# A gated attention/MLP mixer: attention products accumulated in w4's banks, and the gate computed once

## Chip, cores, metric

One core of a Trainium2 chip. The time is device microseconds of one execution on that core; a quoted time is the median of several executions, with the range beside it where it matters.

## The reference, cut

The output mixes a linear attention block A and an MLP block B over 2048 tokens of width 640, token by token, with a sigmoid gate:

```python
g = sigmoid((x * gate_w).sum(-1, keepdims=True))
a = A(x)     # phi(t) = where(t > 0, t + 1, exp(t)) + 1e-6;  o = (phi(q) kv) / (phi(q) z + 1e-6);  o @ wo
b = B(x)     # x1 = x + shift(gelu(LN(x) @ w1)) @ w2;  b = x1 + gelu(LN(x1) @ w3) @ w4
return g * a + (1 - g) * b
```

## The kernel before

The kernel records every operation, puts semaphore waits between the engines, and orders the work by a small timing model of its own: items such as ("k", 13), a key tile, or ("n1", 2), a normalisation, are emitted when the model says that they can run.

Five parts count here. The queries and keys go through `phi`. The clamp, the `ts` line, is a short VectorE operation on bf16 in SBUF:

```python
    def phi(b, dst, after_exp=None):
        se = slot("E", 3)
        src = psf[:, 512 * b:512 * b + D]            # a bank pair of PSUM
        activation(Er[:, se, :], src, ACTF.Exp)
        ...
        ts(dve, Er[:, se, :], Er[:, se, :], 1.0, EPS_PHI, ALU.min, ALU.add)       # the clamp
        return stt(dst, src, 1.0 + EPS_PHI, Er[:, se, :], ALU.add, ALU.max)       # frees the bank pair
```

The gate is computed for four tokens' tiles at a time, after the layer norm statistics of the same four, on ScalarE and GpSimd (POOL). POOL also runs the normalisations:

```python
    def gate_chunk(c):
        cs = slice(4 * c, 4 * c + 4)
        activation(stg[:, 1, cs], lr[:, cs, 1:2]..., ACTF.Tanh, scale=0.5)
        ts(pool, stg[:, 2, cs], stg[:, 1, cs], 0.5, 0.5, ALU.mult, ALU.add)     # g
        ts(pool, stg[:, 3, cs], stg[:, 1, cs], -0.5, 0.5, ALU.mult, ALU.add)    # 1 - g

    def normalize(which, t, st):
        ...
        ts(pool, xn[:, sx, :], x_tok[:, t, :], st[:, 6, t:t + 1], st[:, 7, t:t + 1], ALU.mult, ALU.add)
```

The attention product of a tile is made in a bank pair of its own and evicted at once into `abx`, which already holds (1 - g) x1:

```python
    def a_tile(t):
        ts(pool, abx[:, sa, :], x_tok[:, t, :], stg[:, 3, t:t + 1], 0.0, ALU.mult, ALU.add)
        b = pair()
        mm_group(ps[:, b, 0:512], [... 5 products of 512 columns])
        mm_group(ps[:, b + 1, 0:128], [... 5 products of 128 columns])
        stt(abx[:, sa, :], psf[...], stg[:, 2, t:t + 1], abx[:, sa, :], ALU.mult, ALU.add)
```

The w4 products then go to six fresh banks per chunk of four tiles; their eviction multiplies by 1 - g and adds `abx`. The w3 products of a chunk, 13 groups of five, rotate over all free banks, each group followed by a Gelu on ScalarE that frees its bank. (Cuts are marked with dots.)

Of the kernel before, what the change touches and what calls it, by code (L numbers as in the profile page):

```python
# [8 lines left out]
ALU = mybir.AluOpType  # L9
# [407 lines left out]
def _build(nc, A_x, A_wqkv, A_wo, B_w1, B_w2, B_w3, B_w4, gate_w, out, dbg=None, stop=None):  # L417
# [423 lines left out]
        tt(pool, st[:, 7, cs], st[:, 2, cs], st[:, 6, cs], ALU.mult)  # L841
        ts(pool, st[:, 7, cs], st[:, 7, cs], -1.0, 0.0, ALU.mult, ALU.add)

    def gate_chunk(c):
        cs = slice(4 * c, 4 * c + 4)
        activation(stg[:, 1, cs], lr[:, cs, 1:2].rearrange("p t o -> p (t o)"), ACTF.Tanh, scale=0.5)
        ts(pool, stg[:, 2, cs], stg[:, 1, cs], 0.5, 0.5, ALU.mult, ALU.add)
        ts(pool, stg[:, 3, cs], stg[:, 1, cs], -0.5, 0.5, ALU.mult, ALU.add)

    xn_slots = {}  # L850

# [85 lines left out]

    def stats1(c):
        ln_chunk_stats(st1, c, lr[:, 4 * c:4 * c + 4, 0:1].rearrange("p t o -> p (t o)"))
        gate_chunk(c)  # L940

    for u in range(NT):
        if u % 4 == 0:
            IT.add("S1", ("s1", u // 4), 0.0, lambda u=u: stats1(u // 4), deps=[(("k", u + 3), 1.8)])
        d1 = [(("s1", u // 4), 3.0 + 0.9 * (u % 4))]
        d1.append((("k", 13), 0.0) if u == 0 else (("n1", u - 1), 0.9))
        if u >= 3:
            d1.append((("t1", u - 3), 0.0))
        IT.add("N1", ("n1", u), 0.0, lambda u=u: normalize(1, u, st1), deps=d1)
        IT.add("T1", ("t1", u), 0.0, lambda u=u: t_xn(1, u), deps=[(("n1", u), 1.1)] + ([(("zb",), 0.0)] if u == 12 else []))  # L950
    for u in range(1, NT):
        IT.add("Z", ("z", u), 0.0, lambda u=u: z_add(u), deps=[(("k", NT - 1), 2.0)] if u == 1 else [])
    LAST_EXP = ("k", NT - 1)
# [156 lines left out]

    def qn_scale(t):
        sd = qn_slot[t]
        ts(dve, dnr[:, 0, sd, :], dnr[:, 0, sd, :], EPS_PHI, None, ALU.add, ALU.bypass)
        dve(lambda e: e.reciprocal(dnr[:, 1, sd, :], dnr[:, 0, sd, :]), [dnr[:, 0, sd, :]], [dnr[:, 1, sd, :]], cost=350.0)
        blk = pq_tok[:, t, :].rearrange("p (j c) -> p j c", c=128)
        src = pq_tok[:, t + 1, 0:600].rearrange("p (j c) -> p j c", c=120)
        rec = dnr[:, 1, sd, 0:30].rearrange("p (j a) -> p j a", a=6)
        halves = [(blk[:, :, 68 * e:68 * e + B3].rearrange("p j (a d) -> p j a d", d=DH),
                   src[:, :, 60 * e:60 * e + B3].rearrange("p j (a d) -> p j a d", d=DH),
                   rec[:, :, 3 * e:3 * e + 3].unsqueeze(3).to_broadcast([128, 5, 3, DH]), 450.0) for e in range(2)]  # L1120
        tail = (blk[:, :, 60:68].rearrange("p m (h i) -> p h m i", i=4),
                pq_tok[:, t + 1, 600:D].rearrange("p (h m i) -> p h m i", h=2, i=4),
                dnr[:, 1, sd, 30:32].unsqueeze(2).unsqueeze(3).to_broadcast([128, 2, 5, 4]), 150.0)
        for o, i0, i1, cost in (*halves, tail):
            dve(lambda e, o=o, i0=i0, i1=i1: e.tensor_tensor(o, i0, i1, ALU.mult),  # L1125
                [i0, dnr[:, 1, sd, :]], [o], cost=cost)
# [6 lines left out]
    def a_tile(t):  # L1133
        sa = slot("abx", 4)
        abx_slot[t] = sa
        tag_set("abx", sa, t)
        ts(pool, abx[:, sa, :], x_tok[:, t, :], stg[:, 3, t:t + 1], 0.0, ALU.mult, ALU.add)
        tok = slice(128 * t, 128 * (t + 1))
        b = pair()
        mm_group(ps[:, b, 0:512], [(pqnT[:, j, tok], M_sb[:, j, 0:512]) for j in range(KD)])  # L1140
        mm_group(ps[:, b + 1, 0:128], [(pqnT[:, j, tok], M_sb[:, j, 512:D]) for j in range(KD)])
        stt(abx[:, sa, :], psf[:, 512 * b:512 * b + D], stg[:, 2, t:t + 1], abx[:, sa, :], ALU.mult, ALU.add)

    w4_banks = {}

    def w4_half(t):
        sl = (t // 4) % 2
        tag_chk("h2T", sl, t // 4)
        b0, b2, bt = pair(), pair(), pair()
        tiles = [((b0, b2)[i // 2] + i % 2, bt + i % 2, 128 * (i // 2)) for i in range(4)]  # L1150
        for i in range(4):
            w4_banks[t + i] = tiles[i]
        bank_hold.update((b0, b0 + 1, b2, b2 + 1, bt, bt + 1))

        turned = t < NT - 4

        def fn(e):
            ins = None
            for pr in range(2):
                for par, tail in ((0, False), (1, False)) if turned else ((0, False), (1, False), (0, True), (1, True)):  # L1160
                    rows = slice(64 * par, 64 * par + 64)
                    bm, bs, q0 = tiles[2 * pr + par]
                    l = h2h[rows, t // 4, 128 * pr:128 * (pr + 1)]
                    if tail:
                        ins = e.matmul(ps[:, bs, q0:q0 + 128], l, w4[rows, KFF, 512:D], start=(pr == 0), stop=False,
                                       skip_group_check=True)
                    else:
                        ins = e.matmul(ps[:, bm, :], l, w4[rows, KFF, 0:512], start=True, stop=False)  # L1168
            if turned:
                for par in range(2):  # L1170
                    rows = slice(64 * par, 64 * par + 64)
                    ins = e.matmul(ps[:, bt + par, 0:256], w4[rows, KFF, 512:D], h2h[rows, t // 4, :], start=True, stop=False)  # L1172
            return ins
        pe(fn, [h2h[:, t // 4, :], w4[:, KFF, :]], [ps[:, b, :] for b in (b0, b0 + 1, b2, b2 + 1, bt, bt + 1)], cost=760.0)

    def w4_turned(t):
        sl = (t // 4) % 2
        tag_chk("h2T", sl, t // 4)
        tag_set("mtok", sl, t // 4)
        bt = w4_banks[t][1]  # L1180
        for par in range(2):
            o = ps[:, bt + par, 0:256].rearrange("p (n q) -> p n q", q=128)
            prs = [(w4[:, k, 512:D], h2T[:, sl, k, :].rearrange("p (n h q) -> p n h q", h=2, q=128)[:, :, par, :]) for k in range(KFF)]

            def fn(e, o=o, prs=prs):
                ins = None
                for i, (l, r) in enumerate(prs):
                    ins = e.matmul(o, l, r, start=False, stop=(i == KFF - 1))  # L1188
                return ins
            pe(fn, [x_ for p_ in prs for x_ in p_], [o], cost=KFF * 109.2)  # L1190
            activation(mT[:, sl, :].rearrange("p (n h q) -> p n h q", h=2, q=128)[:, :, par, :], o, ACTF.Copy)
        bank_hold.difference_update((bt, bt + 1))
        sch.dma("sp", mtok[:, sl, :, :], mT[:, sl, :], "trm%d" % sl, transpose=True)

    def w4_tile(t):
        sa = abx_slot[t]
        tag_chk("abx", sa, t)
        sl = (t // 4) % 2
        tag_chk("h2T", sl, t // 4)
        a = t % 4  # L1200
        b1, b2, q0 = w4_banks.pop(t)

        def grp(o, n0, n1):
            prs = [(h2T[:, sl, k, 128 * a:128 * (a + 1)], w4[:, k, n0:n1]) for k in range(KFF)]

            def fn(e):
                ins = None
                for i, (l, r) in enumerate(prs):
                    ins = e.matmul(o, l, r, start=False, stop=(i == KFF - 1), skip_group_check=(n0 > 0))  # L1209
                return ins  # L1210
            pe(fn, [x_ for p_ in prs for x_ in p_], [o], cost=KFF * ((n1 - n0) * 0.4167 + 2.5))
        parts = [(ps[:, b1, 0:512], 0, 512)]
        if t >= NT - 4:
            parts.append((ps[:, b2, q0:q0 + 128], 512, D))
        for o, n0, n1 in parts:
            grp(o, n0, n1)
        bank_hold.discard(b1)
        if t < NT - 4:
            tag_chk("mtok", sl, t // 4)
            parts.append((mtok[:, sl, a, :], 512, D))  # L1220
        elif a >= 2:
            bank_hold.discard(b2)
        for o, n0, n1 in parts:
            stt(x_tok[:, t, n0:n1], o, stg[:, 3, t:t + 1], abx[:, sa, n0:n1], ALU.mult, ALU.add)
# [16 lines left out]
    for c in range(NCH):  # L1241
        for j in range(KD):
            deps = [(("t1", u), 0.9) for u in range(4 * c, 4 * c + 4)] if j == 0 else []
            if c == 0 and j == 0:
                deps.append((LAST_EXP, None))
                deps.append((("ga", KD - 1), None))
            if c == 1 and j == 0:
                deps.append((("g", KD - 1), None))
# [41 lines left out]
                    IT.add("W3", ("w3h", c2), 1.14, lambda c2=c2: w3_half(c2), [(("t2", u), 0.9) for u in range(4 * c2 + 4, 4 * c2 + 8)] + [(("a", 3), 0.0)])  # L1290
                IT.add("W3", ("w4h", 0), 0.76, lambda: w4_half(0), [(("w4load",), 0.0)])
    for t in range(NT):
        deps = [(("zb",), 1.0), (("q", max(t, 2)), 2.0)]
        if t < 7:
            i = (5 * t) // 2 + 3
            deps.append((("w1", i // KD, i % KD), 0.0))
# [9 lines left out]
    for t in range(NT):  # L1306
# [7 lines left out]
        deps4 = [(("a", t), 0.0), (("w3h", c - c % 2), GEL), (("w3", c, KFF - 1), GEL)]  # L1314
        if t % 4 == 0:
            deps4.append((("w3", min(c + 1, NCH - 1), KFF - 1), 0.0))
            if t == 0:
                deps4 = [(("w4h", 0), 0.0)]
        elif t + 3 < NT:
            deps4.append((("a", t + 3), 0.0))  # L1320
# [56 lines left out]
```

## Time and profile before

| | before |
|---|---|
| median of the first three executions | 260.15 us (259.63 to 260.22) |
| span of the profiled execution | 258.4 us |
| TensorE busy | 255.2 us |
| first input product / last w4 product of 512 columns done | 7.15 / 255.69 us |

From the page of before, the busy time of the engines (share of the span, instructions):

```profile
PE 255.2 (99%) x1600; PEld 130.5 (51%) x1600; DVE 151.3 (59%) x290; ACT 109.6 (42%) x223; POOL 93.9 (36%) x152
```

From the same page, the chain of work that ended last, by engine:

```profile
PE 96%; DMA 2%; SPq 0%; DVE 0%; issue 0%
```

A busy TensorE can still stall, so the waits of TensorE itself are the better reading. From the list of waits of before (who waited for whom: total us, times, longest), the longest one of VectorE, and all that the matmuls have; these two lie at the very start:

```profile
DVE x_tok L642 <- PE ps L1209: 62.0, 13, 18.9
...
PE ps L871 <- PEq L1362: 0.8, 1, 0.8
...
PE ps L614 <- DMA x_tok<-in_A_x_dram: 0.2, 1, 0.2
```

So the TensorE is never kept waiting once the first input has landed, and only fewer or cheaper products can shorten the kernel. The groups that the change touches, from the list of groups by shape (line, engine, operation, output and input, count; busy us, mean ns; idle time before):

```profile
L642 DVE SCALAR_TENSOR_TENSOR abx<-ps,stg,abx 128x640 f32<-128x640 f32 x16 | 14.1, 883 | 15.8 <-PE ps L603 8.8 <-POOL abx L625 7.0
L625 DVE TENSOR_SCALAR Er<-Er 128x640 bf16<-128x640 bf16 x32 | 11.6, 363 | 8.1 <-ACT Er L659 8.0
L625 POOL TENSOR_SCALAR stg<-stg 128x4 f32<-128x4 f32 x8 | 1.9, 263 | 0.7 <-ACT stg L659 0.7
L659 ACT ACTIVATE stg<-lr 128x4 f32<-128x4 f32 x4 | 0.8, 203 | 0.0
```

The first goes away, the last two are replaced. The second is not in the change.

```profile
45.79 0.34 POOL L625 TENSOR_SCALAR stg<-stg 128x4 f32<-128x4 f32 x2 [0.50 <-ACT stg L659]
46.07 0.95 POOL L285 DMA_DIRECT2D wv<-in_A_wqkv_dram  x1
47.02 3.28 POOL L285 DMA_DIRECT2D wo_aug<-in_A_wo_dram  x5
50.35 1.80 POOL L625 TENSOR_SCALAR xn<-x_tok,st 128x640 bf16<-128x640 bf16 x2
```

The Gelus of w3 of chunk 2, from the timeline of ScalarE in before (start us, duration us, engine); 0.48 us of idle time between 0.60 us of work:

```profile
175.13 0.60 ACT L659 ACTIVATE h2T<-ps 128x512 bf16<-128x512 f32 x1 [0.48 <-PE ps L603]
176.21 0.60 ACT L659 ACTIVATE h2T<-ps 128x512 bf16<-128x512 f32 x1 [0.48 <-PE ps L603]
```

### The profile page before, as it was taken

The numbers are of one execution on the slowest core, as the hardware profiler recorded it, in microseconds if no ns is written. First come the engines' busy times: TensorE is split into PE (matmuls) and PEld (weight loads), VectorE is DVE, ScalarE is ACT, GpSimd is POOL, SyncE is SP. The second block draws the span as 40 slices with busy tenths as digits, with TensorE's granted clock in tenths as the row PEclk, the third lists the DMA queues.
The fourth block names the chain that finished last, engine by engine and source line by source line (L and its number), as shares of the span: only waits on it lengthen the run. The fifth ranks groups of instructions, "written<-read, shape, count | busy, mean of one in ns | idle before, by whom it ended". The sixth has DMA issues, their size and how long they took to land.

```text
span 258.4 us, 4134 instructions
## 1 busy us (share of the span) xinstructions
PE 255.2 (99%) x1600; PEld 130.5 (51%) x1600; DVE 151.3 (59%) x290; ACT 109.6 (42%) x223; POOL 93.9 (36%) x152
## 2 busy tenths in 40 slices
PE   8999999999999999999999999999999999999996
PEld 3555555544454554555444555444465444644453
DVE  2587877899914999999993403995004410044333
ACT  1496677751366866676854240005510045300000
POOL 5013995969952118767903202222002110012001
PEclk9999999999999999999999999999999999999999
DMA  6764999682764898562825651115010020010211
GB/s 217 215 154 136 208 183 137 178 131 51 100 128 80 152 405 258 65 103 51 105 59 115 123 70 20 28 25 152 0 23 0 0 101 3 0 20 3 103 51 51
DMA packets 54307, 25.86 MB, mean 100 GB/s; under 512 B 45668, under 2 KB 52877, under 8 KB 54288
## 3 DMA queue, kind: packets, MB, share of 16 engines
q1 hardware_dynamic: 52112, 21.21, 37.4%
q0 software_dynamic: 1168, 3.28, 5.7%
q10 hardware_dynamic: 1008, 1.11, 1.2%
q8 instruction: 12, 0.20, 0.3%
q14 instruction: 7, 0.06, 0.1%
HBM read 12.04 MB, written 2.62 MB: 57 GB/s over the span
## 4 chain that ended last, share of the span: by engine, by line
PE 96%; DMA 2%; SPq 0%; DVE 0%; issue 0%
PE ps L603 61%; PE ps L1209 18%; PE ps L805 8%; PE ps L1188 3%; DMA x_tok<-in_A_x_dram 2%; PE ps L898 2%; PE ps L1096 1%; PE ps L1168 1%; SPq L285 0%; PE ps L899 0%; DVE x_tok L642 0%; PE ps L977 0%; PE ps L1006 0%; PE ps L614 0%; PE ps L1172 0%
## 5 line engine op out<-in xcount | busy, mean ns | idle before, releaser
L603 PE MATMUL ps<-xnT,w 128*128 128x512 bf16 x360 | 81.3, 380 | 0.0
L659 ACT ACTIVATE h2T<-ps 128x512 bf16<-128x512 f32 x52 | 30.5, 598 | 60.4 <-PE ps L603 60.4
L603 PEld LDWEIGHTS ps<-xnT,w 128*128 128x128 bf16 x360 | 34.2, 98 | 38.3 <-issue 0.3
L625 POOL TENSOR_SCALAR abx<-x_tok,stg 128x640 f32<-128x640 bf16 x16 | 14.8, 925 | 99.7 <-DVE x_tok L642 94.6
L1209 PE MATMUL ps<-w,h2T 128*128 128x512 bf16 (+1 forms) x260 | 50.1, 348 | 0.0
L642 DVE SCALAR_TENSOR_TENSOR x_tok<-ps,stg,abx 128x512 bf16<-128x512 f32 (+1 forms) x20 | 13.3, 670 | 62.0 <-PE ps L1209 62.0
L625 POOL TENSOR_SCALAR xn<-x_tok,st 128x640 bf16<-128x640 bf16 x32 | 35.3, 1110 | 17.8 <-DMA xnT<-xn 17.3
L1209 PEld LDWEIGHTS ps<-w,h2T 128*128 128x128 bf16 x260 | 22.9, 98 | 22.1 <-issue 0.3
L659 ACT ACTIVATE Er<-ps 128x640 bf16<-128x640 f32 x32 | 22.5, 708 | 15.0 <-PE ps L603 8.0
L658 ACT ACTIVATE junk<-x_tok 128x640 bf16<-128x640 bf16 x32 | 23.6, 739 | 3.4 <-DVE x_tok L640 2.8
L603 PE MATMUL ps<-M_sb,pqnT 128*128 128x512 bf16 (+1 forms) x160 | 24.4, 300 | 0.0
L659 ACT ACTIVATE hsT<-ps 128x512 bf16<-128x512 f32 (+1 forms) x32 | 19.0, 593 | 12.1 <-PE ps L603 11.6
L603 PE MATMUL ps<-w,hsT 128*128 128x512 bf16 (+1 forms) x160 | 23.7, 300 | 0.0
L642 DVE SCALAR_TENSOR_TENSOR abx<-ps,stg,abx 128x640 f32<-128x640 f32 x16 | 14.1, 883 | 15.8 <-PE ps L603 8.8
L603 PE MATMUL ps<-wkg,xT 128*128 128x130 bf16 (+1 forms) x140 | 21.4, 299 | 0.0
L603 PEld LDWEIGHTS ps<-M_sb,pqnT 128*128 128x128 bf16 x160 | 13.6, 98 | 13.0
L603 PE MATMUL ps<-wq,xT 128*128 128x512 bf16 (+1 forms) x130 | 19.8, 300 | 0.0
L603 PEld LDWEIGHTS ps<-w,hsT 128*128 128x128 bf16 x160 | 13.3, 98 | 12.3
L805 PE MATMUL ps<-pk_tok,x_tok 128*128 128x512 bf16 x80 | 17.8, 380 | 0.0
L625 DVE TENSOR_SCALAR Er<-Er 128x640 bf16<-128x640 bf16 x32 | 11.6, 363 | 8.1 <-ACT Er L659 8.0
L1125 DVE TENSOR_TENSOR pq_tok<-pq_tok,dnr 128x300 bf16<-128x300 bf16 (+1 forms) x48 | 15.7, 381 | 0.6
L640 DVE SCALAR_TENSOR_TENSOR x_tok<-ps,x_tok 128x640 bf16<-128x640 f32 x16 | 13.1, 820 | 4.5 <-PE ps L603 3.8
(84 smaller groups left out, 250.6 us busy)
## 6 DMA issues: line engine op xcount, KB each, us to landing
w<-in_B_w_dram SPq DMA_DIRECT2D x1, 2160.0 KB, 8.3
w<-in_B_w_dram SPq DMA_DIRECT2D x1, 2080.0 KB, 13.9
out_dram<-x_tok SPq DMA_DIRECT2D x3, 640.0 KB, 3.1
x_tok<-in_A_x_dram SPq DMA_DIRECT2D x2, 640.0 KB, 5.0
w<-in_B_w_dram POOLq DMA_DIRECT2D x8, 160.0 KB, 4.5
x_tok<-in_A_x_dram SPq DMA_DIRECT2D x5, 160.0 KB, 4.9
wv<-in_A_wqkv_dram POOLq DMA_DIRECT2D x1, 800.0 KB, 6.7
wq<-in_A_wqkv_dram ACTq DMA_DIRECT2D x4, 160.0 KB, 4.1
```

The lines of the kernel that those rows point to most:

```text
L603: ins = e.matmul(out_ap, l, r, start=(i == 0), stop=(i == n - 1))
L625: return engf(lambda e: e.tensor_scalar(out_ap, in_ap, s1, s2, op0, op1), rd, [out_ap], cost=cost)
L640: return dve(lambda e: e.scalar_tensor_tensor(out_ap, in0, scalar, in1, op0, op1, accum_out=accum), rd, [out_ap, accum], cost=cost + 70.0)
L642: return dve(lambda e: e.scalar_tensor_tensor(out_ap, in0, scalar, in1, op0, op1), rd, [out_ap], cost=cost)
L658: return act(lambda e: e.activation(out_ap, in_ap, func, bias=bias, scale=scale, accum_out=accum), rd, wr, cost=cost)
L659: return act(lambda e: e.activation(out_ap, in_ap, func, bias=bias, scale=scale), rd, wr, cost=cost)
L805: ins = e.matmul(o, l, r, start=(t0 + q_ == 0), stop=(t0 + q_ == NT - 1))
L898: e.matmul(ps[:, b, 0:512], l, w[:, k, 0:512], start=(k == 0), stop=(k == KD - 1))
L1096: ins = e.matmul(o, l, r, start=st, stop=sp)
L1125: dve(lambda e, o=o, i0=i0, i1=i1: e.tensor_tensor(o, i0, i1, ALU.mult), [i0, dnr[:, 1, sd, :]], [o], cost=cost)
L1188: ins = e.matmul(o, l, r, start=False, stop=(i == KFF - 1))
L1209: ins = e.matmul(o, l, r, start=False, stop=(i == KFF - 1), skip_group_check=(n0 > 0))
```

## The change

The intent is to save the 16 evictions into `abx`. Since g a + (1 - g)(x1 + h2) = (1 - g)(x1 + h2 + (g / (1 - g)) a), and g / (1 - g) is exp of the gate logit, the queries are scaled by that factor (the denominator is multiplied by exp of minus the logit), the attention products are left in the banks where w4's products accumulate, and one eviction does the rest. The gate itself is then needed late, so its math is done once for all tokens, behind the z sums (the sums of phi(k) over the tokens, for the denominator). The core of the diff:

```diff
-    def gate_chunk(c):                       # per four tiles: Tanh on ACT, two operations on POOL
-        ...
+    def gate_clip():
+        ts(dve, stg[:, 1, :], lr[:, :, 1:2]..., LOGIT, -LOGIT, ALU.min, ALU.max)
+    def gate_exp():
+        activation(stg[:, 2, :], stg[:, 1, :], ACTF.Exp, scale=-1.0)
+    def gate_rest():
+        ts(dve, stg[:, 0, :], stg[:, 2, :], 1.0, None, ALU.add, ALU.bypass)
+        dve(lambda e: e.reciprocal(stg[:, 1, :], stg[:, 0, :]), ...)
+        tt(dve, stg[:, 3, :], stg[:, 2, :], stg[:, 1, :], ALU.mult)
...
     def stats1(c):
         ln_chunk_stats(st1, c, ...)
-        gate_chunk(c)
...
+    IT.add("SG", ("sgc",), 0.0, gate_clip, deps=[(("k", NT - 1), 1.0)])
+    IT.add("SG", ("sg", 0), 0.0, gate_exp, deps=[(("sgc",), 0.2)])
+    IT.add("SG", ("sg", 1), 0.0, gate_rest, deps=[(("z", NT - 1), 0.0)])
...
-        ts(dve, dnr[:, 0, sd, :], dnr[:, 0, sd, :], EPS_PHI, None, ALU.add, ALU.bypass)
+        ts(dve, dnr[:, 0, sd, :], dnr[:, 0, sd, :], EPS_PHI, stg[:, 2, t:t + 1], ALU.add, ALU.mult)
...
     def a_tile(t):
-        b = pair()
-        mm_group(...); mm_group(...)
-        stt(abx[:, sa, :], psf[...], stg[:, 2, t:t + 1], abx[:, sa, :], ALU.mult, ALU.add)
+        b = w4_banks[t] = bank()
+        bank_hold.add(b)                     # held until the last w4 product of this tile
+        acc([(ps[:, b, :], [... 5 products of 512 columns])], True)
+        if t >= NT - 4: ...                  # tails of 128 columns, as before
+        elif i == 3:                         # tails of four tiles, turned: 2 x 5 products of 256 columns
+            ...
...
-                        ins = e.matmul(ps[:, bm, :], l, w4[rows, KFF, 0:512], start=True, stop=False)
+                        ins = e.matmul(ps[:, bm, :], l, w4[rows, KFF, 0:512], start=False, stop=False, ...)
...
+            deps4.append((("a", t + 3), 0.0))        # w4 of a chunk waits for all four attention tiles
```

More of the change, by code (lines that the diff above doesn't have):

```diff
@@ L842, in ln_chunk_stats @@
         ts(pool, st[:, 7, cs], st[:, 7, cs], -1.0, 0.0, ALU.mult, ALU.add)
-    def gate_chunk(c):
-        cs = slice(4 * c, 4 * c + 4)
-        activation(stg[:, 1, cs], lr[:, cs, 1:2].rearrange("p t o -> p (t o)"), ACTF.Tanh, scale=0.5)
-        ts(pool, stg[:, 2, cs], stg[:, 1, cs], 0.5, 0.5, ALU.mult, ALU.add)
-        ts(pool, stg[:, 3, cs], stg[:, 1, cs], -0.5, 0.5, ALU.mult, ALU.add)
+    LOGIT = 60.0
+    def gate_clip():
+        ts(dve, stg[:, 1, :], lr[:, :, 1:2].rearrange("p t o -> p (t o)"), LOGIT, -LOGIT, ALU.min, ALU.max)
+    def gate_exp():
+        activation(stg[:, 2, :], stg[:, 1, :], ACTF.Exp, scale=-1.0)
+    def gate_rest():
+        ts(dve, stg[:, 0, :], stg[:, 2, :], 1.0, None, ALU.add, ALU.bypass)
+        dve(lambda e: e.reciprocal(stg[:, 1, :], stg[:, 0, :]), [stg[:, 0, :]], [stg[:, 1, :]])
+        tt(dve, stg[:, 3, :], stg[:, 2, :], stg[:, 1, :], ALU.mult)
     xn_slots = {}
@@ L1138, in a_tile, with acc, fn @@
         tok = slice(128 * t, 128 * (t + 1))
-        b = pair()
-        mm_group(ps[:, b, 0:512], [(pqnT[:, j, tok], M_sb[:, j, 0:512]) for j in range(KD)])
-        mm_group(ps[:, b + 1, 0:128], [(pqnT[:, j, tok], M_sb[:, j, 512:D]) for j in range(KD)])
-        stt(abx[:, sa, :], psf[:, 512 * b:512 * b + D], stg[:, 2, t:t + 1], abx[:, sa, :], ALU.mult, ALU.add)
+        i = t % 4
+        b = w4_banks[t] = bank()
+        bank_hold.add(b)
+        acc([(ps[:, b, :], [(pqnT[:, j, tok], M_sb[:, j, 0:512]) for j in range(KD)])], True)
+        if t >= NT - 4:
+            if i == 0:
+                for par in range(2):
+                    bt = w4_tails[3, par] = bank()
+                    bank_hold.add(bt)
+            acc([(ps[:, w4_tails[3, i % 2], 128 * (i // 2):128 * (i // 2) + 128],
+                  [(pqnT[:, j, tok], M_sb[:, j, 512:D]) for j in range(KD)])], i < 2)
+        elif i == 3:
+            c = t // 4
+            for par in range(2):
+                bt = w4_tails[c, par] = bank()
+                bank_hold.add(bt)
+                acc([(ps[:, bt, 0:256].rearrange("p (n q) -> p n q", q=128),
+                      [(M_sb[:, j, 512:D], pqnT[:, j, 512 * c:512 * (c + 1)].rearrange("p (n h q) -> p n h q", h=2, q=128)[:, :, par, :])
+                       for j in range(KD)])], True)
+    def acc(groups, first=False, last=False):
+        for o, prs in groups:
+            def fn(e, o=o, prs=prs):
+                ins = None
+                for i, (l, r) in enumerate(prs):
+                    ins = e.matmul(o, l, r, start=first and i == 0, stop=last and i == len(prs) - 1, skip_group_check=True)
+                return ins
+            pe(fn, [x_ for p_ in prs for x_ in p_], [o], cost=len(prs) * (nfree(prs[0][1]) * 0.4167 + 2.5))
+    w4_tails = {}
     w4_banks = {}
@@ L1148, in w4_half @@
         tag_chk("h2T", sl, t // 4)
-        b0, b2, bt = pair(), pair(), pair()
-        tiles = [((b0, b2)[i // 2] + i % 2, bt + i % 2, 128 * (i // 2)) for i in range(4)]
-        for i in range(4):
-            w4_banks[t + i] = tiles[i]
-        bank_hold.update((b0, b0 + 1, b2, b2 + 1, bt, bt + 1))
+        c = t // 4
+        tiles = [(w4_banks[t + i], w4_tails[c, i % 2], 128 * (i // 2)) for i in range(4)]
+        banks = [w4_banks[t + i] for i in range(4)] + [w4_tails[c, par] for par in range(2)]
         turned = t < NT - 4
@@ L1164, in fn @@
                     if tail:
-                        ins = e.matmul(ps[:, bs, q0:q0 + 128], l, w4[rows, KFF, 512:D], start=(pr == 0), stop=False,
+                        ins = e.matmul(ps[:, bs, q0:q0 + 128], l, w4[rows, KFF, 512:D], start=False, stop=False,
                                        skip_group_check=True)
                     else:
-                        ins = e.matmul(ps[:, bm, :], l, w4[rows, KFF, 0:512], start=True, stop=False)
+                        ins = e.matmul(ps[:, bm, :], l, w4[rows, KFF, 0:512], start=False, stop=False, skip_group_check=True)
             if turned:
@@ L1171, in fn @@
                     rows = slice(64 * par, 64 * par + 64)
-                    ins = e.matmul(ps[:, bt + par, 0:256], w4[rows, KFF, 512:D], h2h[rows, t // 4, :], start=True, stop=False)
+                    ins = e.matmul(ps[:, tiles[par][1], 0:256], w4[rows, KFF, 512:D], h2h[rows, t // 4, :], start=False, stop=False,
+                                   skip_group_check=True)
             return ins
-        pe(fn, [h2h[:, t // 4, :], w4[:, KFF, :]], [ps[:, b, :] for b in (b0, b0 + 1, b2, b2 + 1, bt, bt + 1)], cost=760.0)
+        pe(fn, [h2h[:, t // 4, :], w4[:, KFF, :]], [ps[:, b, :] for b in banks], cost=760.0)
     def w4_turned(t):
@@ L1179, in w4_turned @@
         tag_set("mtok", sl, t // 4)
-        bt = w4_banks[t][1]
         for par in range(2):
-            o = ps[:, bt + par, 0:256].rearrange("p (n q) -> p n q", q=128)
-            prs = [(w4[:, k, 512:D], h2T[:, sl, k, :].rearrange("p (n h q) -> p n h q", h=2, q=128)[:, :, par, :]) for k in range(KFF)]
-            def fn(e, o=o, prs=prs):
-                ins = None
-                for i, (l, r) in enumerate(prs):
-                    ins = e.matmul(o, l, r, start=False, stop=(i == KFF - 1))
-                return ins
-            pe(fn, [x_ for p_ in prs for x_ in p_], [o], cost=KFF * 109.2)
+            bt = w4_tails[t // 4, par]
+            o = ps[:, bt, 0:256].rearrange("p (n q) -> p n q", q=128)
+            acc([(o, [(w4[:, k, 512:D], h2T[:, sl, k, :].rearrange("p (n h q) -> p n h q", h=2, q=128)[:, :, par, :]) for k in range(KFF)])],
+                last=True)
             activation(mT[:, sl, :].rearrange("p (n h q) -> p n h q", h=2, q=128)[:, :, par, :], o, ACTF.Copy)
-        bank_hold.difference_update((bt, bt + 1))
+            bank_hold.discard(bt)
         sch.dma("sp", mtok[:, sl, :, :], mT[:, sl, :], "trm%d" % sl, transpose=True)
@@ L1200, in w4_tile @@
         a = t % 4
-        b1, b2, q0 = w4_banks.pop(t)
-        def grp(o, n0, n1):
-            prs = [(h2T[:, sl, k, 128 * a:128 * (a + 1)], w4[:, k, n0:n1]) for k in range(KFF)]
-            def fn(e):
-                ins = None
-                for i, (l, r) in enumerate(prs):
-                    ins = e.matmul(o, l, r, start=False, stop=(i == KFF - 1), skip_group_check=(n0 > 0))
-                return ins
-            pe(fn, [x_ for p_ in prs for x_ in p_], [o], cost=KFF * ((n1 - n0) * 0.4167 + 2.5))
+        b1 = w4_banks.pop(t)
         parts = [(ps[:, b1, 0:512], 0, 512)]
         if t >= NT - 4:
-            parts.append((ps[:, b2, q0:q0 + 128], 512, D))
+            b2 = w4_tails[3, a % 2]
+            parts.append((ps[:, b2, 128 * (a // 2):128 * (a // 2) + 128], 512, D))
         for o, n0, n1 in parts:
-            grp(o, n0, n1)
+            acc([(o, [(h2T[:, sl, k, 128 * a:128 * (a + 1)], w4[:, k, n0:n1]) for k in range(KFF)])], last=True)
         bank_hold.discard(b1)
@@ L1245, in _build @@
                 deps.append((LAST_EXP, None))
+                deps.append((("sg", 0), None))
                 deps.append((("ga", KD - 1), None))
@@ L1292, in _build @@
     for t in range(NT):
-        deps = [(("zb",), 1.0), (("q", max(t, 2)), 2.0)]
+        deps = [(("zb",), 1.0), (("q", max(t, 2)), 2.0), (("sg", 1), 0.0)]
         if t < 7:
```

## The prediction

> **What bounds the kernel now.** The TensorE. The page says busy 255.2 of 258.4 us, but a busy PE may stall, so I read start-to-start times in the timeline: 13 products of 512 columns take 2.80 us (0.216 each), an attention group (five of 512, five of 128) 1.36 us (1.08 + 0.28, so 0.056 per short one), 26 turned products of 256 columns 2.94 us (0.113). The Trainium skill ("TensorE: Matmul & The Clock Gate", "Wait — 56ns, not 53.3ns?") gives 55.6 and 215.7 ns for a warm array; this trace agrees. The chain of waits is 96% PE: from 7.15 us (first input landed) to 255.69 us products back to back. Only about seven steps, where the row layout of the array changes, take 0.31 instead of 0.22 us.
>
> **What the change removes, adds, moves.**
> - TensorE: no column goes. 12 attention groups keep their five 512-column products; their tails turn from 60 products of 128 columns (60 x 0.056 = 3.36 us) into 30 of 256 (3.3 to 3.4 us). Net about zero.
> - VectorE: the 16 evictions into abx go (14.1 us, 883 ns each, by groups). In the w4 stages VectorE waits for PE (62.0 us in the waits), and no product waits for an abx eviction: worth nothing on the chain.
> - Gate: four Tanh (0.8 us of ACT) and eight POOL operations (1.9 us) become one Exp and four small VectorE operations (estimated from the 128x32 ones, 0.25 to 0.35 us: 1 us). Behind the z sums VectorE waits 5.2 us for the z transpose. Table loads stay two: the skill's "ScalarE: Activation LUTs", "Table sets", puts exp and tanh in one set; the groups show two loads. PE is then in GT products. Worth nothing.
> - PSUM: the attention result now holds its bank from the attention product to the last w4 product. In w3 of chunks 2 and 3 six of eight banks are held, so 26 w3 groups (28 us) rotate on two banks. The new hazard: a Gelu starts 0.20 us after its group's last column and takes 0.60: the bank is free 0.80 us after the group; it is needed at 1.08, its first weight load at 0.87. ACT has nothing else there. The slack (0.07 to 0.28 us) is just enough, I think. A later release costs up to 0.1 us per group, at most 2.4 us.
> - Order: w4's half products wait for all four attention tiles. Earlier chunks met that already; tile 15 moves from before w4(15) to before w4(12), and its transposed queries landed at 181 us, long before. No gap.
>
> **On the critical path:** about zero gained, 0 to 2 us at risk.
>
> **Predicted time:** 260.2 us, range 259.3 to 261.5. Faster by over 2%: 1%. Within 2%: 95%. Slower by over 2%: 4%.
>
> **What would show it right.** PE busy near 255 us, span 258 to 259; VectorE down about 13 us to near 138; two table loads; w4 groups at 2.80 us; w3 of chunks 2 and 3 at 14.03 us per 65 products, starts still 0.216 apart. Wrong: steps over 0.26 us every fifth product there, PE or its weight load waiting for ACT's Gelu; or turned attention tails far from 0.11 us each.
>
> **What would make it wrong.** A bank release later than the Gelu's recorded end; a VectorE backlog in chunk 0's w4 (query scaling plus evictions) that delays a held bank; a new order of the early products that opens a gap by the z row or the gate.

## More of the kernel before

```profile
49.49 0.40 DVE L625 TENSOR_SCALAR Er<-Er 128x640 bf16<-128x640 bf16 x1 [0.39 <-ACT Er L659]
49.92 0.82 DVE L642 SCALAR_TENSOR_TENSOR pq_tok<-ps,Er 128x640 bf16<-128x640 f32 x1
50.86 0.55 DVE L625 TENSOR_SCALAR Er<-Er 128x640 bf16<-128x640 bf16 x1
```

These lines of POOL and of VectorE are from the timeline late in the query and key stage: POOL waits 0.50 us for the Tanh, makes the gate, issues six transfers of weights (DMA) and then runs two normalisations. A clamp issued while POOL normalises took 0.55 us; most take 0.33.

## The result

| | before | after |
|---|---|---|
| median, six executions each | 259.85 us (259.07 to 260.22) | 261.03 us (260.33 to 261.79) |
| ratio, 95% interval | | 1.0048 (1.0025 to 1.0071) |
| span of the profiled execution | 258.4 us | 259.6 us |
| VectorE busy | 151.3 us | 141.1 us |

The outputs are correct. The kernel became slower, by half a per cent: small, but the interval leaves out zero.

The answering lines of after: busy times and chain from its page, then the same waits: VectorE's longest and all that the matmuls have.

```profile
PE 254.2 (98%) x1542; PEld 130.9 (50%) x1570; DVE 141.1 (54%) x278; ACT 109.5 (42%) x220; POOL 91.8 (35%) x144
```

```profile
PE 88%; DVE 6%; DMA 2%; ACT 2%; issue 1%; SPq 0%
```

```profile
DVE x_tok L642 <- PE ps L1173: 90.3, 14, 22.1
...
PE ps L878 <- PEq L1381: 0.8, 1, 0.8
PE ps L603 <- DVE pq_tok L642: 0.7, 1, 0.7
...
PE ps L603 <- issue: 0.2, 1, 0.2
PE ps L1173 <- issue: 0.2, 1, 0.2
```

There are 1542 matmuls for 1570 weight loads: 28 matmul records are missing from this trace, and the two waits for "issue" of 0.2 us are such holes. The 0.7 us wait for VectorE's `pq_tok` is none: the weight load before it is late as well, by the list of waits of the weight loads:

```profile
PEld ps L603 <- DVE pq_tok L642: 0.9, 1, 0.9
```

Most of VectorE's 6% in the chain lies between 83 and 96 us, where TensorE loses nothing against before (third and fourth line of the table below). To see where the time went I cut every trace at five weight loads that each kernel has: the first with the key weights, the first of the kv products, the first and last of the products with Lt (kv times wo, in the middle of w1 and w2), and the first of w4's half products.

| stage (us) | before | after | difference, before rounding |
|---|---|---|---|
| start to first key product | 9.86 | 10.22 | +0.36 |
| keys, queries, G products | 66.63 | 67.51 | +0.88 |
| kv, first w1 and w2 products | 16.60 | 16.60 | 0.00 |
| w1, w2, start of w3 | 31.94 | 31.94 | 0.00 |
| w3 | 27.60 | 27.58 | -0.03 |
| first half product of w4 to the end | 105.82 | 105.78 | -0.05 |

The last two stages, which hold all the accumulation work, are 0.07 us shorter together. The first line is the arrival of the first inputs and differs from execution to execution whatever the kernel: it ranged from 9.12 to 11.30 us over all profiles. The second line is the loss. Here is its place, in the chain that ended last in after, between 48 and 53 us (start us, us, what):

```profile
47.94 1.16 PE ps L603 x9
...
49.12 0.71 ACT Er L659
...
49.86 2.02 DVE Er L625
...
51.91 0.84 DVE pq_tok L642
...
52.79 1.54 PE ps L603 x10
```

A key product waits for a bank pair, that waits for the queries' eviction, and that for a clamp of 2.0 us, six times its usual length. The timelines of POOL and then of VectorE in after, at the same place as above:

```profile
45.67 0.95 POOL L285 DMA_DIRECT2D wv<-in_A_wqkv_dram  x1
46.63 3.28 POOL L285 DMA_DIRECT2D wo_aug<-in_A_wo_dram  x5
49.96 2.65 POOL L625 TENSOR_SCALAR xn<-x_tok,st 128x640 bf16<-128x640 bf16 x3
```

```profile
49.86 2.01 DVE L625 TENSOR_SCALAR Er<-Er 128x640 bf16<-128x640 bf16 x1 [0.44 <-ACT Er L659]
51.91 0.82 DVE L642 SCALAR_TENSOR_TENSOR pq_tok<-ps,Er 128x640 bf16<-128x640 f32 x1
52.65 0.32 DVE L625 TENSOR_SCALAR Er<-Er 128x640 bf16<-128x640 bf16 x1
```

Two things changed on POOL. The gate's operations and their wait for the Tanh are gone, so the transfers of weights are issued 0.40 us earlier by the clock, and 0.76 us earlier against the stage, which itself began 0.36 us later (46.07 - 45.67 + 0.36). And three normalisations now stand ahead of the last statistics, not two: the kernel's own timing model saw POOL free earlier and moved one forward.

The groups, for comparison with before: the `abx` evictions are gone, the clamps cost 1.1 us more, and the gate is one Exp and four small VectorE operations.

```profile
L625 DVE TENSOR_SCALAR Er<-Er 128x640 bf16<-128x640 bf16 x32 | 12.7, 397 | 8.0 <-ACT Er L659 7.8
L659 ACT ACTIVATE stg<-stg 128x16 f32<-128x16 f32 x1 | 0.2, 218 | 0.6 <-DVE stg L625 0.6
L633 DVE TENSOR_TENSOR stg<-stg 128x16 f32<-128x16 f32 x1 | 0.4, 363 | 0.0
```

And the Gelus of w3 of chunk 2, on two banks now, at the same rhythm to the hundredth:

```profile
176.33 0.60 ACT L659 ACTIVATE h2T<-ps 128x512 bf16<-128x512 f32 x1 [0.48 <-PE ps L603]
177.41 0.60 ACT L659 ACTIVATE h2T<-ps 128x512 bf16<-128x512 f32 x1 [0.48 <-PE ps L603]
```

### The profile page after: what moved, and what is told of

It reads as the page before. It is cut to its first block, busy times and chain, and to the rows that moved or that the text cites. A ratio compares the mean times of both kernels' runs of the same rounds, so it can differ in the third digit from the quotient of the medians. Undisturbed runs are those within 1.5% of the kernel's fastest.

```text
span 259.6 us, 4019 instructions
## 1 busy us (share of the span) xinstructions
PE 254.2 (98%) x1542; PEld 130.9 (50%) x1570; DVE 141.1 (54%) x278; ACT 109.5 (42%) x220; POOL 91.8 (35%) x144
## 4 chain that ended last, share of the span: by engine, by line
PE 88%; DVE 6%; DMA 2%; ACT 2%; issue 1%; SPq 0%
PE ps L603 45%; PE ps L1173 30%; PE ps L805 8%; DMA x_tok<-in_A_x_dram 2%; PE ps L905 2%; DVE x_tok L640 1%; DVE dnr L1115 1%; ACT hsT L659 1%; PE ps L1105 1%; DVE qprod L633 1%; PE ps L1199 1%; DVE Er L625 1%; DVE pq_tok L1134 1%; SPq L285 0%; PE ps L906 0%
## 5 line engine op out<-in xcount | busy, mean ns | idle before, releaser
L603 PE MATMUL ps<-xnT,w 128*128 128x512 bf16 x349 | 79.8, 379 | 0.5 <-issue 0.2
L642 DVE SCALAR_TENSOR_TENSOR x_tok<-ps,stg,abx 128x512 bf16<-128x512 f32 (+1 forms) x20 | 13.3, 670 | 90.3 <-PE ps L1173 90.3
L1173 PE MATMUL ps<-w,h2T 128*128 128x512 bf16 (+1 forms) x254 | 49.0, 346 | 0.4 <-issue 0.2
L625 POOL TENSOR_SCALAR abx<-x_tok,stg 128x640 f32<-128x640 bf16 x16 | 13.2, 829 | 90.8 <-DVE x_tok L642 90.8
L625 POOL TENSOR_SCALAR xn<-x_tok,st 128x640 bf16<-128x640 bf16 x32 | 36.0, 1133 | 18.4 <-DMA xnT<-xn 18.0
L603 PE MATMUL ps<-w,hsT 128*128 128x128 bf16 (+1 forms) x159 | 23.5, 298 | 0.2
L1173 PE MATMUL ps<-M_sb,pqnT 128*128 128x512 bf16 (+1 forms) x98 | 20.9, 346 | 0.1
L603 PE MATMUL ps<-wq,xT 128*128 128x128 bf16 (+1 forms) x128 | 19.7, 298 | 0.1
L625 DVE TENSOR_SCALAR Er<-Er 128x640 bf16<-128x640 bf16 x32 | 12.7, 397 | 8.0 <-ACT Er L659 7.8
L603 PEld LDWEIGHTS ps<-wkg,xT 128*128 128x128 bf16 x140 | 11.4, 98 | 9.2 <-DVE pq_tok L642 0.9
L633 DVE TENSOR_TENSOR qprod<-qprod,pk_tok 128x640 f32<-128x640 f32 x13 | 15.1, 1164 | 0.4
```

Source lines behind the costliest of these rows:

```text
L603: ins = e.matmul(out_ap, l, r, start=(i == 0), stop=(i == n - 1))
L625: return engf(lambda e: e.tensor_scalar(out_ap, in_ap, s1, s2, op0, op1), rd, [out_ap], cost=cost)
L633: return engf(lambda e: e.tensor_tensor(out_ap, a, b_, op), [a, b_], [out_ap], cost=cost)
L642: return dve(lambda e: e.scalar_tensor_tensor(out_ap, in0, scalar, in1, op0, op1), rd, [out_ap], cost=cost)
L1173: ins = e.matmul(o, l, r, start=first and i == 0, stop=last and i == len(prs) - 1, skip_group_check=True)
```

## The experiments

Theory, called "port theory": the clamp and POOL's normalisations need the same thing. The Trainium skill, "SBUF — State Buffer", section "Who interferes with whom", says that VectorE and GpSimd share one pair of SBUF ports, that a VectorE operation in a two-port fast mode (`tensor_scalar` among them) takes that pair as an exclusive lock, and that the loser blocks fully. With the gate gone from POOL, its normalisations moved into a clamp. Rivals: the accumulation (banks held longer, another order of w4's work) costs the time; the new gate operations themselves do; or it is only the late arrival of the first inputs. All stage figures below are cut as in the table above; "key stage" is its second line.

### The gate half alone

Before, with the gate part of the diff; the old eviction takes the gate from where the new math puts it.

```diff
-        stt(abx[:, sa, :], psf[...], stg[:, 2, t:t + 1], abx[:, sa, :], ALU.mult, ALU.add)
+        stt(abx[:, sa, :], psf[...], stg[:, 1, t:t + 1], abx[:, sa, :], ALU.mult, ALU.add)
```

> Kernel before with the new gate math alone (one Exp, four small VectorE operations); attention products and their evictions as before. Port theory: with the gate's operations gone from POOL, its normalisations start about 0.7 us earlier against the queries' and keys' clamps; one clamp on VectorE takes about 2.0 us instead of 0.33, PE waits about 0.87 us near 52 us for the bank pair behind it, ratio to before 1.003 to 1.007. Accumulation theory (bank holding or the moved order costs the time): no stall there, ratio 0.998 to 1.002. Late-input theory (the first input just landed 0.3 us later): no stall, ratio near 1.000.

Measured: 260.89 us against 259.93 of before, ratio 1.0029 (1.0002 to 1.0055). The key stage took 67.53 us, all others were within 0.01 us of before. The clamp took 2.03 us under three normalisations. The ratio is just under the stated range, the stall is there as expected: the gate half alone carries the loss, and the accumulation is not needed for it.

### The accumulation half alone, two tries

First try: after with the old `gate_chunk`, and one more small multiply per tile to bring the gate in.

```diff
-        ts(dve, dnr[:, 0, sd, :], dnr[:, 0, sd, :], EPS_PHI, stg[:, 2, t:t + 1], ALU.add, ALU.mult)
+        ts(dve, dnr[:, 0, sd, :], dnr[:, 0, sd, :], EPS_PHI, None, ALU.add, ALU.bypass)
         dve(lambda e: e.reciprocal(dnr[:, 1, sd, :], dnr[:, 0, sd, :]), ...)
+        ts(dve, dnr[:, 1, sd, :], dnr[:, 1, sd, :], stg[:, 2, t:t + 1], None, ALU.mult, ALU.bypass)
```

> Kernel after with the old gate math (four Tanh, eight POOL operations); the reciprocal gets one small VectorE multiply by the gate in place of the exp factor. Port theory: POOL runs as before, no clamp over 0.7 us, no PE wait near 52 us, ratio to before 0.998 to 1.002, w3 of chunks 2 and 3 without gaps. Accumulation theory: ratio 1.003 to 1.007, with gaps after 125 us. Late-input theory: near 1.000.

Measured: 260.77 us, ratio 1.0029 (1.0005 to 1.0054), and a wrong result (relative error 0.021), because I scaled by g where g / (1 - g) is needed. The key stage was 66.63 us as in before and no clamp after 30 us took over 0.66 us, but the stage of w1 and w2 took 33.12 us instead of 31.94: PE's weight loads waited in three places near 94, 121 and 126 us, in the first two for VectorE by the trace. VectorE is close to full there (busy 30.6 us of the 32 from 93 us on in before), so I put it down to the added multiply, which the second try leaves out. So this run does not settle the question, and its miss is my edit's. Second try, with the right factor made once:

```diff
+    def gate_odds():
+        dve(lambda e: e.reciprocal(stg[:, 0, :], stg[:, 2, :]), ...)
+        tt(dve, stg[:, 0, :], stg[:, 3, :], stg[:, 0, :], ALU.mult)
...
+        ts(dve, dnr[:, 0, sd, :], dnr[:, 0, sd, :], EPS_PHI, stg[:, 0, t:t + 1], ALU.add, ALU.mult)
```

> The accumulation half alone again, with the right factor this time (gate over one minus gate, made once by two small VectorE operations behind the z sums) and with no operation added per tile. Port theory: POOL runs as before; from the first key product to the first kv product 66.63 us as before, from the first Lt product to the last 31.94 as before (33.12 in the first try), from there to the first half product 27.6, from there to the end 105.78 against 105.82 of before; ratio to before 0.998 to 1.002; correct. Accumulation theory: one of these stages is longer by 0.5 to 1.2 us, ratio 1.003 to 1.007.

Measured: correct, 259.76 us against 260.07, ratio 0.9995 (0.9967 to 1.0024); stages 66.63, 16.60, 31.94, 27.58, 105.78 us. The accumulation half costs nothing and gains 0.06 us by the stages. The accumulation theory falls.

### After, with the old gate's work run besides

This run (after_oldgate_too) adds work and takes nothing away:

```diff
     def stats1(c):
         ln_chunk_stats(st1, c, ...)
+        gate_chunk(c)                # the old one, on a scratch tile stx that nothing reads
```

> Kernel after, complete, with the old gate's Tanh and POOL operations run besides on a scratch tile that nothing reads: work added. Port theory: the added POOL work puts the normalisations back to their old place, the stall goes and the kernel gets faster than after, ratio to before 0.998 to 1.002. Accumulation theory, or any cost of the new gate operations themselves: ratio 1.003 to 1.007 stays.

Measured: 260.18 us against 259.93, ratio 1.0009 (0.9982 to 1.0036), key stage 66.63 us. By the stages useless work made the kernel faster: 248.52 us from the first key product to the end against 249.40 in after (the intervals of the two timed ratios overlap). Its POOL timeline around the same place shows the useless gate, and two normalisations; the line after it, from VectorE's timeline, is the clamp that they now meet:

```profile
45.23 0.34 POOL L626 TENSOR_SCALAR stx<-stx 128x4 f32<-128x4 f32 x2 [0.50 <-ACT stx L660]
...
49.80 1.81 POOL L626 TENSOR_SCALAR xn<-x_tok,st 128x640 bf16<-128x640 bf16 x2
```

```profile
50.29 0.57 DVE L626 TENSOR_SCALAR Er<-Er 128x640 bf16<-128x640 bf16 x1
```

The new gate operations are all still in this kernel, so they are not the cost by themselves; nor is anything else of after.

### Normalisations held back, two ways

First (run after_ordered), each early normalisation waits for the newest clamp at the time it is emitted, and may be emitted only after q tile 14:

```diff
-        d1.append((("k", 13), 0.0) if u == 0 else (("n1", u - 1), 0.9))
+        d1.append((("q", 14), 0.0) if u == 0 else (("n1", u - 1), 0.9))
+        if u in (1, 2):
+            d1.append((("k", 14) if u == 1 else ("q", 15), 0.0))
```

> Kernel after, but the early normalisations on POOL each wait for the end of a clamp on VectorE, so that they run while VectorE reads PSUM and not into a clamp. Port theory: clamps of 45 to 56 us back to 0.33 us or at most 0.9, no PE wait of 0.87 us, span 1 us less than after, ratio to before 0.996 to 1.001. Accumulation theory: ratio 1.003 to 1.007 as after. Late-input theory: near 1.000, whatever POOL does.

Measured: 261.62 us against 259.93, ratio 1.0066 (1.0041 to 1.0091): slower still. The key stage was 66.63 us and its clamps 0.33, as the theory says, but the w1 and w2 stage took 33.70 us. The first normalisation started at 53.58 us instead of about 50; VectorE then waited 7.80 us for the z row's transpose, against 5.24 in before and 2.28 in after, began the query scaling later, and PE's weight loads waited 1.35 us near 95 us and 0.66 near 120. The expected time was wrong because I held the normalisations too long. The second way (run after_timed) names the clamps and keeps the order on all engines exactly that of after:

```diff
+            dp = [clamp_of((pq_tok[:, 15, :], pk_tok[:, 14, :], pq_tok[:, 16, :])[t])]    # q14, k14, q15
...                                          # and three changed dependencies that keep the order
```

> Kernel after with one difference: the three early normalisations on POOL wait for the clamp of q tile 14, k tile 14 and q tile 15 on VectorE. The order on every engine is that of after. Port theory: no clamp above 0.45 us from 45 us on, the stage from the first key product to the first kv product 66.63 us instead of 67.51, all later stages as in after (16.6, 31.94, 27.6, 105.78), ratio to before 0.998 to 1.002 and 0.9 us below after. If the stall comes from anything else, the first stage stays at 67.5. If the normalisations are then too late, the second or third stage grows, as in after_ordered.

Measured: 260.70 us against 260.07, ratio 1.0022 (0.9995 to 1.0049); key stage 66.63 us, the others 16.60, 31.94, 27.58, 105.77. The stages are as expected; the ratio is at the edge, and its first inputs came late in the profile (first key product at 10.51 us against 9.86). POOL and VectorE interleave now, from the two timelines of this run:

```profile
50.59 0.88 POOL L871 TENSOR_SCALAR xn<-x_tok,st 128x640 bf16<-128x640 bf16 x1 [0.38 <-DVE Er L625]
51.95 0.88 POOL L871 TENSOR_SCALAR xn<-x_tok,st 128x640 bf16<-128x640 bf16 x1 [0.48 <-DVE Er L625]
```

```profile
50.15 0.33 DVE L625 TENSOR_SCALAR Er<-Er 128x640 bf16<-128x640 bf16 x1 [0.44 <-ACT Er L659]
...
51.51 0.33 DVE L625 TENSOR_SCALAR Er<-Er 128x640 bf16<-128x640 bf16 x1 [0.18 <-ACT Er L659]
```

From the first key product to the end this kernel needs 248.52 us, before 248.59 and after 249.40. It beats after by these stages; its 0.07 us against before is far below what timed runs can tell.

### The port itself: another instruction for two clamps

If the lock is the cause, an operation that does not take the lock must run through. The clamps of q tile 14 and k tile 14 were replaced by an operation with its second input in PSUM; the skill's same section says that an operation with at most one SBUF input, outside the two-port modes, does not contend. POOL was not touched.

```diff
+        if (dst.tensor.name, dst.offset) in one_port:
+            stt(Er[:, se, :], Er[:, se, :], 1.0, src, ALU.min, ALU.max)
+        else:
             ts(dve, Er[:, se, :], Er[:, se, :], 1.0, EPS_PHI, ALU.min, ALU.add)
```

> Kernel after, POOL untouched (three early normalisations, early start), but the clamps of q tile 14 and k tile 14 are done by another VectorE instruction: minimum with 1 and then maximum with the projection itself, read from PSUM. It gives the same phi (without the 1e-6), has one SBUF input[...] and is slower by itself: about 0.82 us instead of 0.33. Port theory: it runs 0.82 us straight through the normalisations, the bank of q tile 14 is free before PE needs it, first stage 66.6 to 66.9 us instead of 67.5, ratio to before 0.998 to 1.002. If the clamp waits for something else than the port (a semaphore, the Exp before it), it still ends about 2 us after its issue and the stage stays at 67.5 or gets longer.

Measured: 261.13 us against 260.63, ratio 1.0011 (0.9981 to 1.0041), correct, key stage 66.63 us (first inputs at 11.30 us, the latest of all). Its VectorE and then its POOL timeline:

```profile
50.94 0.82 DVE L642 SCALAR_TENSOR_TENSOR Er<-Er,ps 128x640 bf16<-128x640 bf16 x1 [0.44 <-ACT Er L659]
51.79 0.82 DVE L642 SCALAR_TENSOR_TENSOR pq_tok<-ps,Er 128x640 bf16<-128x640 f32 x1
52.53 0.81 DVE L642 SCALAR_TENSOR_TENSOR Er<-Er,ps 128x640 bf16<-128x640 bf16 x1
```

```profile
51.03 2.59 POOL L625 TENSOR_SCALAR xn<-x_tok,st 128x640 bf16<-128x640 bf16 x3
```

Three early normalisations, as in after, and an instruction 2.5 times slower than the clamp by itself; yet the stall is gone. Both engines run at full speed side by side (three normalisations in 2.59 us, 2.65 in after). This agrees with the skill, and it leaves no room for a semaphore or the Exp as the cause. That the thing held is the port pair is the skill's account; what the runs show is that the clamp in its fast form and POOL's normalisations get in each other's way, and that another form of it does not.

### Earlier start or third normalisation?

Both changed at once on POOL. After with the third normalisation put behind the statistics again (run after_two_early):

```diff
+        if u == 2:
+            d1.append((("s1", 3), 0.0))
```

> Kernel after with only two normalisations ahead of the last statistics, as before had, not three; they start as early as in after. If the earlier start is what hurts (port theory), the clamp still waits through two normalisations: about 2.0 us, first stage 67.5 us. If the third normalisation is what hurts, the clamp is short again and the stage is 66.6. The z row may come later (as in after_ordered), which would lengthen the third stage by up to 2 us.

Measured: 260.42 us (one execution), clamp 1.17 us, key stage 66.67 us, the later stages as in after. I had expected 2.0 us and 67.5: wrong. With one normalisation fewer behind it, the clamp, which again was issued (49.90 us) just before the first normalisation (50.01), waited through one of them and not two. The mirror image, before with three:

> Kernel before, old gate and all, with one thing moved: three normalisations on POOL ahead of the last statistics, not two. If the third one is what makes a clamp wait through a whole normalisation more (what after_two_early showed), the clamp that took 0.55 us in before (it was issued during the first normalisation) takes about 1.45 us; it falls on a key tile, so PE may lose anything from 0 to 0.5 us: first stage 66.6 to 67.2. If the earlier start of POOL is needed as well, the clamp stays at 0.55 and the stage at 66.63.

```diff
-        IT.add("S1", ("s1", u // 4), ..., deps=[(("k", u + 3), 1.8)])
+        IT.add("S1", ("s1", u // 4), ..., deps=[(("k", u + 3), 1.8)] + ([(("n1", 2), 0.0)] if u == 12 else []))
```

Measured: 260.27 us (one execution), two clamps of 0.74 and 0.82 us, key stage 66.63 us. The third normalisation alone costs nothing, against the 1.45 us that I expected of one clamp. Then after (run after_again) and the version with two, timed in the same rounds:

> Kernel after, unchanged, in the same rounds as the version with two early normalisations. Clamp of 2.0 us, first stage 67.5 us, ratio to before 1.003 to 1.006.

> Kernel after with two normalisations ahead of the last statistics, timed now. Clamp 1.17 us, first stage 66.7 us; ratio to before 0.998 to 1.002, about 0.8 us under after_again.

Measured: after 261.00 us against 260.04, ratio 1.0041 (1.0012 to 1.0070), key stage 67.53 us. With two early normalisations 260.12 us, ratio 1.0009 (0.9981 to 1.0037), but in this profile a key stage of 67.14 us, where the same kernel had 66.67 in the profile before. This loss has another cause: at 44.20 us, before any normalisation, a weight load waited for a transposed input that came late, and no product of the stage waits for a clamp (those of 0.90 and 0.61 us included). The only wait of the weight loads from 10 to 76 us, from the list of waits:

```profile
PEld ps L603 <- DMA xT<-x_tok: 0.7, 1, 0.7
```

So the full loss needs both: the earlier start, and three normalisations in a row. With both, every profile shows 67.51 to 67.54 us (four profiles). With the start alone it is 0.04 us in the one profile without that late input; with the third alone (one profile), nothing.

### One bank for w3

The hazard that I had predicted, the two banks of w3, cost nothing. How near was it? After, with w3 of chunks 2 and 3 on a single bank:

```diff
-        b = bank()
+        b = w3_bank[c] = bank() if c < 2 or j == 0 else w3_bank[c]
```

> Kernel after with w3 of chunks 2 and 3 on one bank instead of the two that are free. It measures how late a bank comes free. My estimate from the trace: Gelu ends 0.80 us after its group's last column; with the hand-over a group then takes 1.95 to 2.1 us instead of 1.08, 24 of 26 groups pay 0.87 to 1.0 us, in all 21 to 24 us, ratio about 1.08 to 1.095. A bank that came free later than 1.08 us after its group (period above 2.16) would mean that two banks stall as well; the trace of after shows none.

Measured: 281.65 us (one execution), the last stage 126.51 us instead of 105.78: 20.73 us over 24 groups, 0.86 each, just under what I had expected. From its timeline, two groups:

```profile
180.78 0.60 ACT L659 ACTIVATE h2T<-ps 128x512 bf16<-128x512 f32 x1 [1.35 <-PE ps L603]
181.43 0.76 PEld L603 LDWEIGHTS ps<-xnT,w 128*128 128x128 bf16 x5 [1.18 <-ACT h2T L659]
181.43 1.25 PE L603 MATMUL ps<-xnT,w 128*128 128x512 bf16 x5 [0.69 <-ACT h2T L659]
182.72 0.60 ACT L659 ACTIVATE h2T<-ps 128x512 bf16<-128x512 f32 x1 [1.34 <-PE ps L603]
```

A group takes 1.94 us (182.72 - 180.78) instead of 1.08, and the next weight load starts 51 ns after the Gelu's recorded end (181.374 to 181.425 in the trace). In after a Gelu ends 67 ns before the first weight load of the group after next, which needs its bank (175.849 and 175.916 us), so I estimate that two banks leave about 16 ns until the weight load would move, and some 0.2 us until the product would. It fits, narrowly.

## Why the prediction was right or wrong

- **What bounds the kernel, and the accumulation: right.** No column went and nothing on the chain was saved: the stages with the attention and w4 products changed by -0.07 us together. The 14.1 us of evictions, and the 15.8 us that VectorE had waited before them, became waiting: its wait for PE rose from 62.0 to 90.3 us.
- **The turned tails: right.** They were put at 3.3 to 3.4 us against 3.36, "net about zero"; ten turned tails of after start 0.109 us apart, so 30 are about 3.3 us, and the last stage, which has two of the three sets, became 0.05 us shorter.
- **The two banks: right that they are just enough.** The 65 products of w3 of chunk 2 took 14.03 us (174.13 to 188.16 in the chain). The release takes 51 ns.
- **Two table loads: right.** Before, which runs both exp and tanh, shows two (1283 ns each), which agrees with the skill's "Table sets" on exp and tanh; after, without tanh, shows two as well.
- **The gate, "worth nothing": wrong, and the step that failed.** I costed the gate's POOL operations (1.9 us) as work that nobody waits for, and asked only what the new operations meet (PE is then in GT products), not what POOL does earlier without the old ones. What the runs showed: taking them away lets POOL's normalisations start 0.76 us earlier against the stage and lets a third one follow directly, and together they hold up a clamp of VectorE for 1.68 us (2.01 against the usual 0.33). Some 0.80 us of that is slack of the bank pair, 0.88 us reaches PE. With those 0.88 us and the -0.07, the sum is 0.81 us (from the first key product to the end, 249.40 - 248.59).
- **VectorE near 138 us: missed.** It was 141.1. The forecast took off the evictions (14.1 us) and put on the gate (1.0), but not what else grew: 1.1 us of longer clamps, 0.5 us of slower z sums (16.0 against 15.4 us), and 1.1 us in the query scaling (37.5 against 36.4).
- **The time: 260.2 us predicted, 261.03 measured**, inside 259.3 to 261.5 and "within 2%". The range held by luck: it had room for a stall elsewhere (0 to 2 us at risk for the two banks), not because I saw this one. "A new order of the early products that opens a gap by the z row or the gate" was listed as a way to be wrong; it was the order and the timing on POOL, not that of the products.

Open: the measured difference (ratios of 1.0048 and 1.0041) comes to about 0.25 to 0.45 us more than the 0.81 us that the stages show. The intervals cover 0.81, and the arrival of the first inputs varies by more than that, but no run isolates the rest. The timed ratios still sort by the stall: the three kernels that have it (after twice, the gate half alone) came out at 1.0029 to 1.0048, each interval above 1; the five that lack it, and lost nothing elsewhere by their edit, at 0.9995 to 1.0022, each interval with 1 in it. Open too is by what rule the port pair is handed over: why a clamp issued just before the row loses to two normalisations out of three, but to one out of two, while in before with three a clamp issued during the first (51.43 us) ended at 52.17, before the second did (52.84).

## What to carry to other kernels

An operation on an idle engine may be holding apart two others: before calling its removal free, ask what starts earlier when it is gone, which resource that takes, and what is on the critical path just then. When a change has several parts, cut both traces into the same stages at instructions that both have; here that put all the loss that the stages show into one stage in which the main part of the change does no work, and runs with one part each, or with the useless old work added back, confirmed it. Do so for every profile: a second profile of one kernel lost 0.5 us in the same stage for another reason. And an instruction that is slower alone can be the faster one if it keeps off a contended port.

## What the Trainium skill lacked or had wrong

- "SBUF — State Buffer", "Who interferes with whom": it says that whoever issues first gets the port pair for the whole instruction. Here the clamp started by its record at 49.860 us, while POOL was still issuing a transfer of weights (until 49.910); the normalisation that started at 49.956 went ahead of it, and so did the next one at 50.82. The clamp ended at 51.87. With only two normalisations in a row (1.17 us) it lost to one. Who held the pair at 49.860 the record does not show, so it does not prove the page wrong. How a waiting VectorE operation fares against POOL operations that follow each other directly stands nowhere.
- Same page, "SBUF: two separate sides": the trap with descriptors written by GpSimd is told as VectorE holding up the transfer. The other direction may exist, but is not shown: a clamp took 0.65 us instead of 0.33 at 46.50 us in before, beside POOL's issue of transfers of weights, while those at 46.87 and 48.23 us in after, beside the same issue, took 0.33.
- Same page, "Who interferes with whom": the rule on which operation keeps off the lock has no duration beside it, and holds here. The two-input operation with one input in PSUM took 0.82 us beside three normalisations of 0.87 us each.
- No page that I read gives the time from the end of a ScalarE instruction to the first weight load that waits for it; the run on one bank shows 51 ns.
